# The first products of an all-expert layer as Strassen's seven block products over pairs of token chunks

## The chip, the cores and the metric

The kernel runs on one core of one Trainium2 chip. The metric is the time of the whole launch on the device, in microseconds (us), as the median of several runs. The engines are called PE (TensorE, matrix products), ACT (ScalarE), DVE (VectorE), POOL (GpSimd) and SP (SyncE, which issues most DMAs). PEld is PE's weight load, which runs beside its matmuls.

## What is computed

Three layers, one after the other: windowed attention with a linear bias, a layer in which each token goes to one of eight experts of limited capacity, and a layer in which each token goes through all of four experts. The change touches the last one:

```python
# x: [2304, 512], p: [2304, 4], w1: [4, 512, 1024], w2: [4, 1024, 512]
p = domain_probs / (domain_probs.sum(-1, keepdims=True) + 1e-09)
out = np.zeros((N, D), dtype=np.float32)
for e in range(E):
    h = np.maximum(x @ w1[e], 0.0)
    out += p[:, e:e + 1] * (h @ w2[e])
```

`x @ w1[e]` are the first products here, `h @ w2[e]` the second products.

## The kernel before

**A product in three.** PE multiplies in a reduced fp32 format (fp32r). So each fp32 matrix is kept as a high and a low part: ACT rounds to the high part, and POOL or DVE subtracts it from the whole to get the low part. `mm3` then issues three matmuls, high x high, high x low and low x high, into one PSUM bank.

**Stages.** Attention runs to about 155 us, the routed layer with its eight groups (`grp[g]`, 288 tokens each) to about 610 us, the all-expert layer from 621 us on. Through the group stage a planner sets the order: each piece of work is a `step(name, engine, us, function, needs, rank)`, and `arranged` lays the steps on the engines by their needs, assumed lengths and ranks. The tokens' vectors y of the routed layer go to `y_dram`, as a high and a low part (`out_y`, L1013). Part of the all-expert layer is done inside the group stage, as fill: the first six of eight hidden tiles of expert 0 (`NFF = 6`; tiles `hp_f`, `po_f`; results `pt`, kept in `part_dram`, L1075 and L1082). Also there, eight pieces of the next stage's weights are loaded and split on ACT and DVE (`next w`).

**The turn.** The step `turn` closes the group stage's pools and opens the pool for the columns: `columns` loads y back from `y_dram` (L1107), and `sums` loads what `part_dram` holds as the first value of the sums `acc` (L1111). All tokens' columns (`yTh`, `yTl`) and all sums then stay in SBUF.

**The all-expert stage.** The remaining 26 hidden tiles of 128 are seven units, `UNITS` = (expert, first tile, tiles): six units of four tiles and one of two. The outer loop goes over the units, the inner over six chunks of `CH = 384` tokens. For each chunk, `hid_mm` makes each of the unit's hidden tiles (`hp_b`: four steps of 128 rows, three matmuls each), `hid_up` (L800) evicts the relu of it on ACT as the high part, `hid_lo` (L803) the low part on DVE; then `combine` makes the second products of the chunk before (`po`, 128 tokens x 512) and adds them to `acc` on DVE, times the token's share (L1211). Two weight pieces of the next unit are split with every chunk, high on ACT (L755), low on POOL (L760), so each weight is split once. In the last unit each finished block of 128 tokens is scattered to its rows by a DMA from POOL's queue (L1213). In this stage PE and ACT follow the order in which the code is written (`tc.manual_schedule`); DVE, POOL and SP are ordered by the scheduler.

Of the kernel before, what the change touches and what calls it, by code (L numbers as in the profile page):

```python
# [25 lines left out]
def fused_kernel(ctx: ExitStack, tc: tile.TileContext, q, k, v, w_gate, w1, w2, probs, m2w1, m2w2, out, dbg=None):  # L26
# [27 lines left out]
    y_dram = dram.tile([P, 2, NK, NT], F32, name="y_dram")  # L54
# [470 lines left out]
    wp = ctx.enter_context(tc.tile_pool(name="wp", bufs=2))  # L525
# [203 lines left out]
    jobs, raws = [], []  # L729

# [59 lines left out]
    def mm3(o, ah, al, bh, bl, first, last):  # L790
        T.matmul(o, ah, bh, start=first, stop=False)  # L791
        T.matmul(o, ah, bl, start=False, stop=False)  # L792
        T.matmul(o, al, bh, start=False, stop=last)  # L793
# [95 lines left out]
    def pieces(n, job_of, known, free, names):  # L889
        nonlocal npieces  # L890
        for j in range(n):
            i = npieces
            npieces += 1
            raw = {}
            step(
                ("load", i), SP_, 0.5, lambda j=j, raw=raw: raw.update(r=load_piece(job_of(j))),
                [known, ("low", i - NRAW) if i >= NRAW else None, ("load", i - 1) if i else None], 3,
            )
            step(
                ("up", i), ACT_, 0.54, lambda j=j, raw=raw: upper_piece(job_of(j), raw["r"]),  # L900
                [(("load", i), LAND), free(j), ("up", i - 1) if i else None], 3,
            )
            step(("low", i), DVE_, 0.6, lambda j=j, raw=raw: lower_piece(V, job_of(j), raw["r"]), [("up", i), ("low", i - 1) if i else None], 3)
            names.append(("low", i))
# [23 lines left out]
    for g in range(E):  # L928
# [8 lines left out]
        for c in range(NK):  # L937
            def rows(g=g, c=c):
# [12 lines left out]
                [("rows", g, c), (("out", g - 1), 5.0) if g else None], 1,  # L951
# [30 lines left out]
        for i in range(NK):  # L982
            for f in range(2 * NFH):
                hf, ff = f // NFH, f % NFH

                def outputs(g=g, i=i, f=f, hf=hf, ff=ff):
                    d = grp[g]
                    if f == 0:
                        d["yp", i] = ps_y.tile([P, 512], F32, tag="y", name=f"y_{g}_{i}")
                    (wh, wl), (hh, hl) = d["w", hf][1][0], d["h", hf]  # L990
                    dsl = slice(i * P, (i + 1) * P)
                    mm3(d["yp", i][:, :CAP], wh[:, ff, dsl], wl[:, ff, dsl], hh[:, ff, :CAP], hl[:, ff, :CAP], f == 0, f == 2 * NFH - 1)
                step(
                    ("y", g, i, f), PE_, 0.41, outputs,
                    [prev_pe, ("hl", g, hf, ff), names[8 + f], bank(banks_y, 2, ("yl", g, i)) if f == 0 else None], 3,
                )
# [93 lines left out]
    CH = 384  # L1090
    NCH = NT // CH
    yT, accs = [None] * NCH, [None] * NCH
    accp = []

    def late_pool(name, side, columns_of, sums_of):
        pool = ctx.enter_context(tc.tile_pool(name=name, bufs=1, side=side, reuse_waits="tile"))
        accp.append(pool)
        for ch in columns_of:
            yT[ch] = [pool.tile([P, NK, CH], F32R, name=f"yT{n}_{ch}") for n in "hl"]
        for ch in sums_of:  # L1100
            accs[ch] = pool.tile([P, CH // P, DM], F32, name=f"acc_{ch}")

    def columns(ch):

        cs = slice(ch * CH, (ch + 1) * CH)
        for n in range(2):
            nc.sync.dma_start(yT[ch][n].bitcast(F32), y_dram[:, n, :, cs])  # L1107
# [8 lines left out]
    pieces(  # L1116
        8, lambda j: (w0["n"][0][1] + w0["n"][1][1])[j], ("next w",),
        lambda j: ("hid", E - 1, 0, NFH - 1, NK - 1) if j < 4 else ("y", E - 1, NK - 1, 2 * NFH - 1), [],
    )

    def turn():
        rctx.close()
        hctx.close()
        late_pool("acca", "right", range(4), range(1))

    step(("turn",), SP_, 0.0, turn, [("first h", E - 1, NFF - 1, NK - 1), ("fl", E - 1, NFF - 1), ("out", E - 1), ("keep", E - 1), ("gather", E - 1)], 1)
    for ch in range(2):
        step(("columns", ch), SP_, 0.8, lambda ch=ch: columns(ch), [("turn",), (("out", E - 1), 6.0)], 2)
# [59 lines left out]
    late_pool("accb", "left", range(4, NCH), range(1, NCH))  # L1188
    sums(0)
    for ch in range(2, NCH):  # L1190
        columns(ch)
        sums(ch - 1)
    sums(NCH - 1)


# [4 lines left out]
    done, stores = [], []  # L1200

    def combine(u, ch, w, h):
        e, _, nf = UNITS[u]
        for i in range(CH // P):
            t = ch * (CH // P) + i
            po = ps_y.tile([P, 512], F32, tag="y", name=f"po_{u}_{t}")
            ts_ = slice(i * P, (i + 1) * P)
            for f in range(nf):
                mm3(po, h[0][:, f, ts_], h[1][:, f, ts_], w[2][:, f, :], w[3][:, f, :], f == 0, f == nf - 1)
            pe = pp[:, t, e : e + 1]  # L1210
            V.scalar_tensor_tensor(accs[ch][:, i, :], po, pe, accs[ch][:, i, :], ALU.mult, ALU.add)  # L1211
            if u == len(UNITS) - 1:
                st = G.indirect_dma_start(  # L1213
                    out=out, out_offset=bass.IndirectOffsetOnAxis(ap=ids[:, t : t + 1], axis=0),
                    in_=accs[ch][:, i, :], in_offset=None,
                )
                for other in stores:
                    tc.declare_no_dep(st.ins, other.ins, reason="rows of other tokens")
                stores.append(st)

    ctx.enter_context(tc.manual_schedule(engines={mybir.EngineType.PE, mybir.EngineType.Activation}))
    unit = w0["n"]
    for u, (_, _, nf) in enumerate(UNITS):
        w = unit[0][0] + unit[1][0]
        for ch in range(NCH):
            h = [accp[0].tile([P, NFH, CH], F32R, tag=f"h{n}", name=f"h{n}_b{u}_{ch}", bufs=2) for n in "hl"]
            for f in range(nf):
                hp = ps_h.tile([P, 512], F32, tag="h", name=f"hp_b{u}_{ch}_{f}")
                for c in range(NK):
                    hid_mm(hp, w[:2], yT[ch], f, c, CH)  # L1230
                hid_up(hp, h, f, CH)
                hid_lo(hp, h, f, CH)
            done.append((u, ch, w, h))
            if len(done) > 1:
                combine(*done[-2])

            if ch == 0 and u + 1 < len(UNITS):
                unit = all_w(*UNITS[u + 1])
                jobs.extend(unit[0][1] + unit[1][1])
            for _ in range(min(2, len(jobs))):  # L1240
                split_piece()
# [29 lines left out]
```

## Time and profile before

| | us |
|---|---|
| runs | 1284.18, 1284.43, 1285.84 |
| median | 1284.43 |
| the profiled execution | 1281.37 |
| its span (first to last instruction) | 1279.7 |
| PE busy in it | 1224.9 |
| DVE, ACT, POOL busy | 633.8, 403.8, 216.6 |

The rows come from the profiled execution, so sums are made against 1281.37. An engine's busy time counts its own instructions; a matmul's duration in the timeline overlaps the next one's, so a pace is read from the starts.

### The profile page before, as it was taken

What the parts mean: (1) busy time and instruction counts of PE and PEld (TensorE: products, weight loads), DVE (VectorE), ACT (ScalarE), POOL (GpSimd) and SP (SyncE); (2) the same over time, 40 slices, a digit from 0 to 9 for tenths busy, and PEclk for the clock granted to TensorE, in tenths of its full rate; (3) what the DMA queues carried; (4) which work ended last, traced back from release to release, by engine and by line L of the source; (5) the groups of instructions that cost most, each with busy time, mean ns of one, the idle gap of its engine ahead of it and who ended that gap; (6) DMA issues with size and microseconds to landing.
All of it is one profiled execution on the core that took longest, in us unless ns stands there. A gap on an engine that the chain in (4) does not pass through costs nothing.

```text
span 1279.7 us, 21264 instructions
## 1 busy us (share of the span) xinstructions
PE 1224.9 (96%) x8209; PEld 1108.0 (87%) x8209; DVE 633.8 (50%) x1828; ACT 403.8 (32%) x1041; POOL 216.6 (17%) x264
## 2 busy tenths in 40 slices
PE   7999828999999999999999999999999999999998
PEld 6998817888889899999999889889999998888896
DVE  6999888898868564433122243222222222222222
ACT  8998733433233243433211112111111111111110
POOL 8867500100000000000100111101101100100112
PEclk9999957999999999999999999999999999999999
DMA  9653144544444253544940111101100000000111
GB/s 182 150 144 76 51 150 101 172 121 111 133 139 148 74 161 109 164 136 121 324 179 1 33 34 33 33 1 33 32 2 17 34 17 17 9 1 1 41 42 66
DMA packets 125012, 108.58 MB, mean 85 GB/s; under 512 B 76272, under 2 KB 91632, under 8 KB 124912
## 3 DMA queue, kind: packets, MB, share of 16 engines
q1 hardware_dynamic: 121936, 97.76, 26.9%
q0 software_dynamic: 2976, 9.48, 2.2%
q8 instruction: 64, 1.05, 0.3%
q14 instruction: 36, 0.29, 0.1%
HBM read 83.53 MB, written 23.68 MB: 84 GB/s over the span
## 4 chain that ended last, share of the span: by engine, by line
PE 69%; DVE 10%; issue 5%; DMA 2%; POOL 1%; ACT 0%; POOLq 0%; SPq 0%; DVEq 0%; ACTq 0%
PE hp_b L791 8%; PE hp_b L793 8%; PE hp_b L792 8%; PE po L791 8%; PE po L793 8%; PE po L792 7%; PE hp_a L791 2%; PE hp_a L792 2%; PE hp_a L793 2%; PE po_f L791 2%; DMA raw_a<-in_moe_w_dram 2%; DVE wl_a L760 2%; PE y L791 2%; PE po_f L792 2%; PE po_f L793 2%
## 5 line engine op out<-in xcount | busy, mean ns | idle before, releaser
L800 ACT ACTIVATE hh_b<-hp_b 128x384 fp32r<-128x384 f32 x156 | 76.6, 491 | 535.9 <-PE hp_b L793 535.9
L803 DVE SCALAR_TENSOR_TENSOR hl_b<-hp_b,hh_b 128x384 fp32r<-128x384 f32 x156 | 87.0, 558 | 263.9 <-ACT hh_b L800 263.9
L793 PE MATMUL hp_b<-yTh,wl_b 128*128 128x384 f32 x624 | 209.6, 336 | 0.0
L791 PE MATMUL hp_b<-yTh,wh_b 128*128 128x384 f32 x624 | 209.6, 336 | 0.0
L792 PE MATMUL hp_b<-yTl,wh_b 128*128 128x384 f32 x624 | 209.4, 336 | 0.0
L1211 DVE SCALAR_TENSOR_TENSOR acc<-po,pp,acc 128x512 f32<-128x512 f32 x126 | 94.6, 751 | 219.0 <-PE po L793 219.0
L791 PE MATMUL po<-wh_b,hh_b 128*128 128x512 f32 x468 | 184.8, 395 | 0.0
L793 PE MATMUL po<-wh_b,hl_b 128*128 128x512 f32 x468 | 184.7, 395 | 0.0
L792 PE MATMUL po<-wl_b,hh_b 128*128 128x512 f32 x468 | 184.7, 395 | 0.0
L760 POOL TENSOR_TENSOR wl_b<-raw_b,wh_b 128x512 fp32r<-128x512 f32 x44 | 56.0, 1291 | 536.2 <-ACT wh_b L755 439.8
L791 PEld LDWEIGHTS hp_b<-yTh,wh_b 128*128 128x128 f32 x624 | 117.3, 188 | 1.8
L792 PEld LDWEIGHTS hp_b<-yTl,wh_b 128*128 128x128 f32 x624 | 117.3, 188 | 1.7
L793 PEld LDWEIGHTS hp_b<-yTh,wl_b 128*128 128x128 f32 x624 | 117.3, 188 | 0.0
L793 PEld LDWEIGHTS po<-wh_b,hl_b 128*128 128x128 f32 x468 | 87.8, 188 | 21.3
L792 PEld LDWEIGHTS po<-wl_b,hh_b 128*128 128x128 f32 x468 | 87.8, 188 | 19.5
L791 PEld LDWEIGHTS po<-wh_b,hh_b 128*128 128x128 f32 x468 | 87.7, 187 | 19.4
L760 DVE TENSOR_TENSOR wl_a<-raw_a,wh_a 128x512 fp32r<-128x512 f32 x128 | 84.0, 682 | 2.3 <-ACT wh_a L755 1.7
L721 POOL DMA_INDIRECT xg<-x_dram,idx x24 | 24.5, 1019 | 356.0 <-DMA p_dram<-xg 55.1
L755 ACT CAST wh_a<-raw_a 128x512 fp32r<-128x512 f32 x128 | 72.6, 619 | 29.8 <-DMA raw_a<-in_moe_w_dram 29.5
L791 PE MATMUL hp_a<-xh,wh_a 128*128 128x288 f32 x256 | 80.4, 314 | 0.0
L791 PE MATMUL y<-hh_a,wh_a 128*128 128x288 f32 x256 | 78.3, 306 | 0.5 <-DVE yl L1006 0.3
L792 PE MATMUL hp_a<-xl,wh_a 128*128 128x288 f32 x256 | 76.4, 298 | 0.0
(219 smaller groups left out, 2502.5 us busy)
## 6 DMA issues: line engine op xcount, KB each, us to landing
raw_a<-in_moe_w_dram SPq DMA_DIRECT2D x128, 256.0 KB, 3.7
raw_b<-in_moe_w_dram SPq DMA_DIRECT2D x64, 256.0 KB, 2.7
x_dram<-x SPq DMA_DIRECT2D x18, 258.0 KB, 2.5
y_dram<-yh SPq DMA_DIRECT2D x8, 576.0 KB, 3.1
y_dram<-yl SPq DMA_DIRECT2D x8, 576.0 KB, 4.8
yTh<-y_dram SPq DMA_DIRECT2D x6, 768.0 KB, 9.5
yTl<-y_dram SPq DMA_DIRECT2D x6, 768.0 KB, 11.0
acc<-part_dram SPq DMA_DIRECT2D x6, 768.0 KB, 11.2
```

The costliest lines, as they stand in the source:

```text
L721: G.indirect_dma_start(out=xg[:, j, :], out_offset=None, in_=x_dram[:, :], in_offset=bass.IndirectOffsetOnAxis(ap=d["idx"][:, j : j + 1], ...
L755: S.copy(res[n][0][0][:, a, b], raw)
L760: eng.tensor_tensor(lo[:, a, b], raw, hi[:, a, b].bitcast(F32), ALU.subtract)
L791: T.matmul(o, ah, bh, start=first, stop=False)
L792: T.matmul(o, ah, bl, start=False, stop=False)
L793: T.matmul(o, al, bh, start=False, stop=last)
L800: S.activation(h[0][:, f, :n], hp[:, :n], AF.Relu)
L803: V.scalar_tensor_tensor(h[1][:, f, :n], hp[:, :n], 0.0, h[0][:, f, :n].bitcast(F32), ALU.max, ALU.subtract)
L1211: V.scalar_tensor_tensor(accs[ch][:, i, :], po, pe, accs[ch][:, i, :], ALU.mult, ALU.add)
```

## The change

The first products of the all-expert stage are regrouped. Two chunks of 384 tokens form a pair, and a product of a unit is read as a 2x2 block product: the hidden tiles in two halves, the 512 rows of the contraction in two halves, the pair's two chunks. Strassen's scheme makes it from seven products of sums and differences of blocks instead of eight products of blocks. The outer loop is now over the three pairs, the inner over the units, there and back, which gives 21 turns. The seven products of a turn accumulate in three kinds of PSUM banks (`m1`, `m2`, `m3`), and behind each stands one block of 128 tokens of the second products of the turn before (`second_products`); six such blocks, so the seventh product has none behind it.

What is prepared: per pair, `token_work` loads four blocks of y, makes four sums or differences of them (`t1` to `t4`) on DVE, and splits seven operands (ACT and DVE, 768 columns). Per unit within a pair, `weight_work` loads four blocks of w1, makes `s1` to `s4` on POOL, splits seven operands (ACT high, POOL low), and loads and splits the second weights (`vh`, `vl`; ACT and POOL). At the two changes of the pair the unit stays the same, so its weights are used again; 19 of the 21 turns have new ones. The part of the preparation with slot i is written behind product i of the turn before. For the first turn it is steps of the planner behind the step `turn`.

What else goes with it: `y_dram` holds y once, in fp32, for which ACT makes a copy `ys`; the steps `next w` and `columns` are gone; `wp` and two PSUM pools now close at the turn; `acc` has three buffers and is loaded pair by pair.

```diff
-    y_dram = dram.tile([P, 2, NK, NT], F32, name="y_dram")
+    y_dram = dram.tile([P, NK, NT], F32, name="y_dram")
...
+                    d["ys"] = fw.tile([P, NK, CAP], F32, tag="ys", name=f"ys_{g}")
...
+            step(("ys", g, i), ACT_, 0.42, lambda g=g, i=i: S.copy(grp[g]["ys"][:, i, :], grp[g]["yp", i][:, :CAP]), [("yh", g, i), (("out", g - 1), 5.0) if g else None], 2)
...
-            for n in range(2):
-                nc.sync.dma_start(y_dram[:, n, :, g * CAP : (g + 1) * CAP], grp[g]["y"][n].bitcast(F32))
-        step(("out", g), SP_, 1.0, out_y, [(("yl", g, NK - 1), 0.5)], 2)
+            nc.sync.dma_start(y_dram[:, :, g * CAP : (g + 1) * CAP], grp[g]["ys"])
+        step(("out", g), SP_, 0.6, out_y, [(("ys", g, NK - 1), 0.3), ("yl", g, NK - 1)], 2)
...
-    step(("next w",), SP_, 0.0, start_w("n", lambda: all_w(*UNITS[0])), [("load", npieces - 1)], 1)
...
-    for ch in range(2):
-        step(("columns", ch), SP_, 0.8, lambda ch=ch: columns(ch), [("turn",), (("out", E - 1), 6.0)], 2)
...
+        l = {kj: load(*kj) for kj in ((0, 0), (1, 1), (0, 1), (1, 0))}
+        x0 = split(0, (0, 0), [l[0, 0]])
+        t3 = less("t3", (1, 1), (0, 1), ALU.subtract, [l[1, 1], l[0, 1]], 0)
+        t1 = less((0, 1), (0, 1), (0, 0), ALU.subtract, [t3, l[0, 0]], 0)
+        t2 = less((0, 0), "t3", (0, 0), ALU.add, [t1, x0], 1)
+        split(1, (0, 0), [t2])
+        x2 = split(2, (1, 0), [l[1, 0]])
+        split(3, "t3", [t2])
+        split(4, (0, 1), [t1])
+        t4 = less((1, 0), (1, 0), (0, 0), ALU.subtract, [x2, t2], 5)
+        split(5, (1, 0), [t4])
+        split(6, (1, 1), [t3])
...
+        l = {ik: load(*ik) for ik in ((0, 0), (1, 0), (1, 1), (0, 1))}
+        x0 = split(0, (0, 0), [l[0, 0]])
+        s1 = less("s1", (1, 0), (1, 1), ALU.add, [l[1, 0], l[1, 1]], 0)
+        s3 = less((1, 0), (0, 0), (1, 0), ALU.subtract, [s1, l[0, 0]], 0)
+        s2 = less((0, 0), "s1", (0, 0), ALU.subtract, [s3, x0], 1)
+        split(1, (0, 0), [s2])
+        x2 = split(2, (0, 1), [l[0, 1]])
+        split(3, (1, 0), [s3])
+        split(4, "s1", [s2])
+        split(5, (1, 1), [s1])
+        s4 = less((0, 1), (0, 1), (0, 0), ALU.subtract, [x2, s2], 6)
+        split(6, (0, 1), [s4])
+        for f in range(nf):
+            second_piece(f)
...
+    first = {}
+    for what, (todo, made) in (("t", token_work(0)), ("w", weight_work(0, "0"))):
+        first[what] = made
+        for i, (eng, us, fn, needs, _) in enumerate(todo):
+            lands = [(((what, j)), LAND) if todo[j][0] == SP_ else (what, j) for j in needs]
+            step((what, i), eng, us, fn, [("turn",), *lands], 3)
...
+        product(0, 1, True)
+        s1 = {}
+        for f in range(nh):
+            s1[f] = temp("s1", f)
+            S.copy(s1[f], m[1, f][:, :CH])
+        yield
+        product(1, 2, True)
+        u2 = plus("u2", 2, s1)
+        yield
+        product(2, 1, False)
+        result({f: m[1, f] for f in range(nh)}, 0, 0)
+        yield
+        product(3, 2, False)
+        u3 = plus("u3", 2, s1)
+        yield
+        product(4, 3, True)
+        result(plus("cs", 3, u3), 1, 1)
+        yield
+        product(5, 2, False)
+        result(plus("cs", 2, s1), 1, 0)
+        yield
+        product(6, 3, False)
+        result(plus("cs", 3, u2), 0, 1)
+        yield
...
+        for i, _ in enumerate(first_products(u, pair, w[0], x, h, str(n))):
+            next(before_, None)
+            for slot, fn in work:
+                if slot == i:
+                    fn()
```

In this cut `product(i, bank, new)` issues 2 x 3 matmuls for each of the unit's `nh` tiles of one half into bank `m1`, `m2` or `m3`, either anew or onto what it holds; `plus` is a DVE sum of a bank and an SBUF tile; `result(a, i, j)` is `hid_up` and `hid_lo` for half i of chunk j.

The order of the instructions shows where this stands on two engines. In the names, the last numbers only tell tiles apart; `pt_7_1` and `pt_7_2` are the last evictions of the group stage's fill, `hh_b0_0` those of the first unit. On ACT at the turn, before:

```order
L1075 ACTIVATE pt_7_1_9710<-po_f7_1_9684,ppf_7_1_9339 128x512
L1075 ACTIVATE pt_7_2_9728<-po_f7_2_9706,ppr_7_9342 128x512
L800 ACTIVATE hh_b0_0_9768<-hp_b0_0_0_9770 128x384
L800 ACTIVATE hh_b0_0_9768<-hp_b0_0_1_9785 128x384
L800 ACTIVATE hh_b0_0_9768<-hp_b0_0_2_9800 128x384
L800 ACTIVATE hh_b0_0_9768<-hp_b0_0_3_9815 128x384
```

The same place on ACT after the change (`xh` the seven token operands, `wh0_0` the first weight operand of turn 0):

```order
L1063 ACTIVATE pt_7_1_9725<-po_f7_1_9683,ppf_7_1_9357 128x512
L1118 CAST xh2_0_9730<-b10_0_9676 128x768
L1118 CAST xh6_0_9738<-b11_0_9669 128x768
L1118 CAST xh4_0_9747<-b01_0_9671 128x768
L1118 CAST xh1_0_9755<-b00_0_9662 128x768
L1063 ACTIVATE pt_7_2_9763<-po_f7_2_9719,ppr_7_9360 128x512
L1118 CAST xh3_0_9765<-t3_0_9723 128x768
L1118 CAST xh5_0_9773<-b10_0_9676 128x768
L1162 CAST wh0_0_9777<-a00_0_9681 128x512
```

Six token casts and the first weight cast now stand behind or between the evictions `pt`. A little further on ACT after the change, from turn 0's second copy `s1` to its first evictions `hh` (`wh0_1`, `wh1_1`, `wh2_1` are operands of turn 1):

```order
L1335 COPY s1_0_1_9864<-m1_0_1_9855 128x384
L1162 CAST wh6_0_9812<-a01_0_9703 128x512
L1174 CAST vh2_0_9821<-w2raw2_0_9816 128x512
L1174 CAST vh3_0_9825<-w2raw3_0_9819 128x512
L1162 CAST wh0_1_9874<-a00_1_9866 128x256
L1162 CAST wh1_1_9900<-a00_1_9866 128x256
L787 ACTIVATE hh_0_0_9844<-m1_0_0_9848 128x384
L787 ACTIVATE hh_0_0_9844<-m1_0_1_9855 128x384
L1162 CAST wh2_1_9920<-a01_1_9872 128x256
```

Five weight casts stand ahead of the two `hh` of product 2, the last of them of the next turn's sums. On POOL behind the group stage's last gather, before:

```order
L760 TENSOR_TENSOR wl_b06_0_9839<-raw_b06_0_0_0_9830,wh_b06_0_9838 128x2x256
L760 TENSOR_TENSOR wl_b06_0_9839<-raw_b06_0_2_0_9832,wh_b06_0_9838 128x2x256
L760 TENSOR_TENSOR wl_b06_1_9949<-raw_b06_1_0_0_9834,wh_b06_1_9948 128x512
L760 TENSOR_TENSOR wl_b06_1_9949<-raw_b06_1_1_0_9836,wh_b06_1_9948 128x512
L760 TENSOR_TENSOR wl_b14_0_10455<-raw_b14_0_0_0_10444,wh_b14_0_10454 128x512
```

And after the change (`L1155` the sums of weight blocks, where `s2` overwrites `a00` and `s4` overwrites `a01`; `L1164` and `L1177` the low parts):

```order
L1155 TENSOR_TENSOR s1_0_9742<-a10_0_9689,a11_0_9694 128x512
L1155 TENSOR_TENSOR a10_0_9689<-a00_0_9681,a10_0_9689 128x512
L1164 TENSOR_TENSOR wl0_0_9778<-a00_0_9681,wh0_0_9777 128x512
L1155 TENSOR_TENSOR a00_0_9681<-s1_0_9742,a00_0_9681 128x512
L1164 TENSOR_TENSOR wl2_0_9782<-a01_0_9703,wh2_0_9781 128x512
L1164 TENSOR_TENSOR wl1_0_9801<-a00_0_9681,wh1_0_9800 128x512
L1164 TENSOR_TENSOR wl3_0_9787<-a10_0_9689,wh3_0_9786 128x512
L1164 TENSOR_TENSOR wl4_0_9804<-s1_0_9742,wh4_0_9803 128x512
L1164 TENSOR_TENSOR wl5_0_9790<-a11_0_9694,wh5_0_9789 128x512
L1155 TENSOR_TENSOR a01_0_9703<-a01_0_9703,a00_0_9681 128x512
L1177 TENSOR_TENSOR vl0_0_9794<-w2raw0_0_9708,vh0_0_9793 128x512
L1164 TENSOR_TENSOR wl6_0_9813<-a01_0_9703,wh6_0_9812 128x512
```

Before, POOL's first work here belonged to the second unit; now it is the first turn's own weights, one operation after another.

## Rows read from the trace of the kernel before

**Rows 1.** Of the page: the span, and busy us (share) xinstructions of each engine

```profile
span 1279.7 us, 21264 instructions
PE 1224.9 (96%) x8209; PEld 1108.0 (87%) x8209; DVE 633.8 (50%) x1828; ACT 403.8 (32%) x1041; POOL 216.6 (17%) x264
```

**Rows 2.** Groups by line: xcount | busy us, mean ns | idle before, releaser

```profile
L793 PE MATMUL hp_b<-yTh,wl_b 128*128 128x384 f32 x624 | 209.6, 336 | 0.0
...
L793 PE MATMUL po<-wh_b,hl_b 128*128 128x512 f32 x468 | 184.7, 395 | 0.0
...
L800 ACT ACTIVATE hh_b<-hp_b 128x384 fp32r<-128x384 f32 x156 | 76.6, 491 | 535.9 <-PE hp_b L793 535.9
...
L803 DVE SCALAR_TENSOR_TENSOR hl_b<-hp_b,hh_b 128x384 fp32r<-128x384 f32 x156 | 87.0, 558 | 263.9 <-ACT hh_b L800 263.9
...
L1211 DVE SCALAR_TENSOR_TENSOR acc<-po,pp,acc 128x512 f32<-128x512 f32 x126 | 94.6, 751 | 219.0 <-PE po L793 219.0
...
L760 POOL TENSOR_TENSOR wl_b<-raw_b,wh_b 128x512 fp32r<-128x512 f32 x44 | 56.0, 1291 | 536.2 <-ACT wh_b L755 439.8
...
L760 DVE TENSOR_TENSOR wl_a<-raw_a,wh_a 128x512 fp32r<-128x512 f32 x128 | 84.0, 682 | 2.3 <-ACT wh_a L755 1.7
...
L755 ACT CAST wh_a<-raw_a 128x512 fp32r<-128x512 f32 x128 | 72.6, 619 | 29.8 <-DMA raw_a<-in_moe_w_dram 29.5
```

**Rows 3.** Timeline of PE at both ends of the stage; start us, duration us

```profile
620.76 0.39 PE L793 MATMUL po_f<-wh_b,restl 128*128 128x512 f32 x1
620.99 0.34 PE L791 MATMUL hp_b<-yTh,wh_b 128*128 128x384 f32 x1
...
1272.92 0.40 PE L793 MATMUL po<-wh_b,hl_b 128*128 128x512 f32 x1
```

**Rows 4.** Timeline of PE within that stage, first products and second products

```profile
700.35 0.33 PE L791 MATMUL hp_b<-yTh,wh_b 128*128 128x384 f32 x1
...
700.87 0.33 PE L791 MATMUL hp_b<-yTh,wh_b 128*128 128x384 f32 x1
...
705.21 0.40 PE L791 MATMUL po<-wh_b,hh_b 128*128 128x512 f32 x1
...
705.91 0.39 PE L791 MATMUL po<-wh_b,hh_b 128*128 128x512 f32 x1
```

**Rows 5.** Timeline of SP's queue and a window (columns as in Rows 7) at the turn

```profile
608.52 0.38 SPq L1107 DMA_DIRECT2D yTh<-y_dram  x1
...
613.00:615.00 2.00, 2.00 (x11) 1.61 (x10) 0.00 (x0) 0.51 (x1) 0.00 (x0) 1.00 1.03 362
```

**Rows 6.** Timeline of ACT at the turn; in brackets the idle time before

```profile
616.99 0.69 ACT L1075 ACTIVATE pt<-po_f,ppf 128x512 f32<-128x512 f32 x1 [3.47 <-PE po_f L793]
621.19 0.69 ACT L1075 ACTIVATE pt<-po_f,ppr 128x512 f32<-128x512 f32 x1 [3.51 <-DMA part_dram<-pt]
```

**Rows 7.** Windows: busy us (instructions) by engine, granted clock, DMA

```profile
core 0: us, PE busy (x) PEld busy (x) DVE busy (x) ACT busy (x) POOL busy (x), PEclk, DMA share, GB/s
...
160.00:165.00 5.00, 1.30 (x19) 1.01 (x19) 3.63 (x13) 1.24 (x2) 0.00 (x0) 0.64 0.78 254
200.00:205.00 5.00, 5.00 (x25) 4.53 (x24) 4.45 (x14) 1.96 (x5) 0.00 (x0) 0.50 0.45 131
205.00:210.00 5.00, 5.00 (x40) 4.61 (x39) 3.48 (x11) 2.14 (x5) 0.00 (x0) 0.92 0.63 36
```

**Rows 8.** The same windows view, for the middle of the group stage

```profile
200.00:560.00 360.00, 352.14 (x2710) 320.49 (x2709) 256.28 (x763) 129.96 (x290) 20.89 (x21) 0.99 0.43 129
```

**Rows 9.** Line 457 (min/median/max ns), then DVE's and POOL's timelines at 96 us

```profile
L457 DVE TENSOR_SCALAR rs<-sums x36: 156/393/726, 14.1 to 153.7; 128x4 f32<-128x4 f32 x36
...
96.49 1.15 DVE L122 TENSOR_TENSOR eq<-logits,m 128x72 f32<-128x72 f32 x1
...
96.26 1.28 POOL L350 TENSOR_TENSOR vl<-v,vh 128x512 fp32r<-128x512 f32 x1
```

More of the change, by code (lines that the diff above doesn't have):

```diff
@@ L788, in all_w, with mm3 @@
         )
[L790 to L793, printed above, removed]
+    def mm3(o, ah, al, bh, bl, first, last, onto=False):
+        kept = dict(skip_group_check=True) if onto else {}
+        T.matmul(o, ah, bh, start=first, stop=False, **kept)
+        T.matmul(o, ah, bl, start=False, stop=False, **kept)
+        T.matmul(o, al, bh, start=False, stop=last, **kept)
     def hid_mm(hp, w, x, f, c, n):
@@ L950, in fused_kernel @@
                 ("xh", g, c), ACT_, 0.42, lambda g=g, c=c: S.copy(grp[g]["x"][0][:, c, :], grp[g]["tp", c][:, :CAP]),
-                [("rows", g, c), (("out", g - 1), 5.0) if g else None], 1,
+                [("rows", g, c)], 1,
             )
@@ L994, in fused_kernel @@
                     ("y", g, i, f), PE_, 0.41, outputs,
-                    [prev_pe, ("hl", g, hf, ff), names[8 + f], bank(banks_y, 2, ("yl", g, i)) if f == 0 else None], 3,
+                    [prev_pe, ("hl", g, hf, ff), names[8 + f], bank(banks_y, 2, ("ys", g, i)) if f == 0 else None], 3,
                 )
@@ L1090, in fused_kernel @@
     CH = 384
[L1091 to L1107, printed above, removed]
@@ L1121, in turn, with late_pools @@
-    def turn():
+    NPAIR = NT // (2 * CH)
+    ORDER = ("11", "s2t2", "12", "s3t3", "s1t1", "a22t4", "s4b22")
+    UNITS = [(1, 0, NFH), (0, NFF, 2 * NFH - NFF), (1, NFH, NFH)] + [(e, f, NFH) for e in range(2, E2) for f in (0, NFH)]
+    dp = {}
+    def late_pools():
         rctx.close()
         hctx.close()
-        late_pool("acca", "right", range(4), range(1))
-    step(("turn",), SP_, 0.0, turn, [("first h", E - 1, NFF - 1, NK - 1), ("fl", E - 1, NFF - 1), ("out", E - 1), ("keep", E - 1), ("gather", E - 1)], 1)
@@ new lines, in fused_kernel @@
+    step(("turn",), SP_, 0.0, late_pools, [("first h", E - 1, NFF - 1, NK - 1), ("fl", E - 1, NFF - 1), ("out", E - 1), ("keep", E - 1), ("gather", E - 1)], 1)
+    first = {}
[4 more added lines that the diff above has]
+            step((what, i), eng, us, fn, [("turn",), *lands], 3)
@@ L1187, in fused_kernel @@
     fctx.close()
[L1188 to L1193, printed above, removed]
+    dl = ctx.enter_context(tc.tile_pool(name="dl", bufs=1, reuse_waits="tile"))
     ids = moe.tile([P, NTL], I32, name="ids")
@@ L1199, in fused_kernel @@
     nc.sync.dma_start(pp, p_dram.rearrange("(t p) e -> p t e", p=P))
-    done, stores = [], []
-    def combine(u, ch, w, h):
-        e, _, nf = UNITS[u]
[L1204 to L1241, printed above, removed]
@@ L1242, in fused_kernel, with sums, second_products @@
-    combine(*done[-1])
+    ctx.enter_context(tc.manual_schedule(engines={mybir.EngineType.PE, mybir.EngineType.Activation}))
+    stores, accs = [], {}
+    def sums(ch):
+        cs = slice(ch * CH, (ch + 1) * CH)
+        accs[ch] = dl.tile([P, CH // P, DM], F32, tag="acc", name=f"acc_{ch}", bufs=3)
+        nc.sync.dma_start(accs[ch], part_dram[cs, :].rearrange("(t p) d -> p t d", p=P))
+    def second_products(u, pair, second, h, last):
+        e, _, nf = UNITS[u]
+        for j in range(2):
+            ch = 2 * pair + j
+            for i in range(CH // P):
+                t = ch * (CH // P) + i
+                po = ps_y.tile([P, 512], F32, tag="y", name=f"po_{u}_{t}")
+                ts_ = slice(i * P, (i + 1) * P)
+                for f in range(nf):
+                    mm3(po, h[j][0][:, f, ts_], h[j][1][:, f, ts_], second[f][0], second[f][1], f == 0, f == nf - 1)
+                pe = pp[:, t, e : e + 1]
+                V.scalar_tensor_tensor(accs[ch][:, i, :], po, pe, accs[ch][:, i, :], ALU.mult, ALU.add)
+                if last:
+                    st = G.indirect_dma_start(
+                        out=out, out_offset=bass.IndirectOffsetOnAxis(ap=ids[:, t : t + 1], axis=0),
+                        in_=accs[ch][:, i, :], in_offset=None,
+                    )
+                    for other in stores:
+                        tc.declare_no_dep(st.ins, other.ins, reason="rows of other tokens")
+                    stores.append(st)
+                yield
@@ L1246 @@
+    for _ in before_:
+        pass
 _INS = ['q', 'k', 'v', 'moe_w_gate', 'moe_w1', 'moe_w2', 'moe2_domain_probs', 'moe2_w1', 'moe2_w2']
```

143 lines of the change are left out of this document (119 added, 24 removed).

## The prediction, made before the changed kernel had run

> **What bounds the kernel now.** First the page: in a span of 1279.7 us PE is busy 1224.9, 96% [rows 1]. Then the groups by line: the first products of the all-expert stage (hp_b, three times 624 matmuls) and its second products (po, three times 468) show no idle time before them, while the eviction on ACT (hh_b) waited 535.9 us for PE [rows 2]. Next the bounds of the stage on PE: the last group-stage matmul is followed by the first hp_b at 620.99 without a gap, and the last po starts at 1272.92 [rows 3]. The pace there: from 700.35 to 700.87 three hp_b matmuls, 0.52/3 = 0.1735 us each; from 705.21 to 705.91 three po matmuls, 0.2333 each [rows 4]. Check: 1872 x 0.1735 + 1404 x 0.2333 = 324.8 + 327.6 = 652.4 us, which is 620.99 to 1273.3. So this stage is matmul count times pace and nothing else; PE at a granted clock of 1.00 is its only limit, and only fewer matmuls shorten it.
>
> **What is removed.** Strassen leaves seven block products of eight: 1872 x 7/8 = 1638 matmuls of 384 columns. 234 x 0.1735 = **40.6 us** off PE. The second products keep their count and shape. The new matmuls have the same 128x128 weights and 384 columns, so I keep the pace.
>
> **The steady state of the new loop.** There are 21 turns (7 units x 3 token pairs). A full turn is 7 x 2 x 2 x 3 = 84 first and 6 x 4 x 3 = 72 second matmuls: 14.6 + 16.8 = 31.4 us of PE. A short turn comes three times, and the mean over 21 is (284.2 + 327.6)/21 = 29.1. Against that, per full turn:
> POOL: 4 sums and 11 splits of 128x512, 1.291 us each as in the wl_b row [rows 2]: 19.4 us. Weights were split once, 44 pieces on POOL in the whole stage; now 19 of 21 turns prepare theirs.
> DVE: 10 sums out of PSUM and 8 hl, each at the hl_b row's 0.558, and 6 acc at 0.751: 14.6 us; at the two pair changes some 10 more for token blocks (11 operations of 768 columns; the wl_a row's 0.682 for 512 gives 1.0 at most, I take 0.9).
> ACT: 11 weight casts at 0.619, 8 hh and 2 copies at 0.491: 11.7 us.
> All stay below 29.1, POOL as the nearest with 10 us to spare, and PE's order puts a chunk of second products (2.8 us) behind each product (2.1 us), which covers the 1.05 us from a product's end through hh and hl, or 1.6 us with the sum before them. So I cost these at nothing; the cover is gone if one POOL operation takes over 29.1/15 = 1.94 us.
>
> **The first turn is not covered, and this is the large cost.** Before, the split weights of the first unit were ready at the turn: they lay in the group stage. Now token loads, weight loads, sums and splits start at the turn step, where the column loads started, 608.52 [rows 5]. PE still has 12.4 us of the last po_f until 620.99.
> Loads: four token blocks of 393 KB, four weight blocks of 256 KB, then part_dram and two second pieces, 2.6 to 3.2 MB. At 362 GB/s, what the column loads moved [rows 5], that is 7 to 9 us: landed by 616 to 619. Not the limit.
> ACT's hand-written order is. The cast wh0 stands behind pt_7_2, which ran at 621.19 for 0.69 us [rows 6] (its row names a DMA as releaser, but PE's last po_f ended only at 621.15 [rows 3]), and behind two token casts of 768 columns. From 0.619 for 512 [rows 2] I take 0.88 for 768 (bounds 0.62 and 0.93). So wh0 ends at 621.88 + 1.76 + 0.62 = 624.3, wl0 on POOL 625.6; behind it POOL works one piece after another at 1.29 (s2, wl2, wl1 at 629.5, ... s4 634.6, vl0 635.9, wl6 637.2, vl1 638.5). Product 1 needs wl1, so it ends at about 631 and product 6 at 641.4, against 635.5 had PE gone on from 620.9: 5.9 us lost.
> Then ACT again: hh of product 2 stands behind wh6, vh2, vh3 and the next unit's wh0 and wh1. vh3 wants a load whose buffer vl1 frees at 638.5; wh0 of the next turn a load behind acc, 768 KB, about 644; wh1 the fourth of four POOL operations of 256 columns, which at 0.73 (between half of 1.29 and the whole) end at 647.3. Then hh and hl, 648.8. Only then is a PSUM bank free for turn 1's first product. Its product and the first chunk, which also needs hh of product 5 (two slots further in ACT's queue), end at about 654.7; undisturbed this would be 620.9 + 14.6 + 1.0 + 2.8 = 639.3. Lost: **15.4 us**.
> Clock: PE then stands for several us at a time. After PE was busy 1.30 of 5 us the granted clock was 0.64; with PE full at 200 to 205 it was 0.50 and then 0.92 in the next 5 [rows 7]. Half speed for the first 5 us and 0.8 of the next 5 (0.92) loses **2.9 us**; bounds 0 (the waits here may leave the clock alone) and 5.8 (twice).
> Sum 18.3 us. From below: 4 us, if the order of the casts delays only the first product (624.3 less 620.9). From above: 30, if each of the 19 POOL operations that stand in a row takes 0.6 us more.
>
> **Other edits.** In the group stage y is stored once instead of as hi and lo: 16 stores of 576 KB become 8, ACT gets 32 copies (under the hh_b row's 0.491, since they have 288 columns; inside waits of ACT for PE), the eight weight pieces for the next stage leave DVE. PE is busy 352.1 of 360 us there [rows 8], so at most 8 us could come back, and none of the edits takes a matmul out. The planner's order on PE changes a little: 0, bounds -4 to +4. If the ACT copies hold up the evictions, a y bank comes free later, and that is inside these 4. The tail after the last po, 1272.92 to 1279.7, keeps its scatter of six chunks: 0.
>
> **Sum.** -40.6 + 18.3 = -22.3. The profiled execution took 1281.37, of which the span is 1279.7; it is 3.06 under the median of the runs, 1284.43. So 1259.1 for the profiled one, **1262.1** for the median.
>
> **Rivals.**
> *The first turn is mostly hidden.* If ACT's casts come through sooner than I read the queue (the pt waits shorter, the loads for turn 1 ahead of acc) only the late start is lost, 4 us: -36.6, 1248. For it: DVE and POOL are idle at the turn, and the loads land before PE ends. Against: ACT's order is fixed by hand, and pt_7_2 waits for PE.
> *Small stalls in each turn.* POOL's chain and ACT's queue couple turns: hl of the last products, or wh1 ahead of hh, may keep PE 0.3 to 0.7 us a turn. 21 x 0.5 = 10.5: 1272.5. For: hh of product 2 stands behind the next wh1, which waits for three POOL sums. Against: these have 10 us of slack in a turn of 29.
> *POOL becomes the bound, and it is slower.* The rows show DVE and POOL in each other's way: a DVE operation that has both inputs in SBUF, 128x72, took 1.15 us and ended 0.1 us after the POOL operation that began before it; and a 128x4 one took from 156 to 726 ns [rows 9]. If this also works the other way, so that each POOL operation waits for one DVE operation of 0.751, it costs 1.291 + 0.75 = 2.04 us, 15 of them 30.6, over the deciding 29.1. With 1.5 us x 19 turns = 29 more: 1291. Against: in that same row the POOL operation kept its 1.28 us; it was DVE that paid, and 14.6 us of DVE in 29.1 can bear it; of its 24 operations a turn only the six hl that read the sums have both inputs in SBUF.
> The Trainium skill, page "Advanced Engine Details and Errata", section "VectorE Performance Modes", says that the second SBUF port of Vector is shared with GPSIMD and that the instructions "will interfere/block eachother". The 1.15 us row bears out the blocking of DVE; that POOL is blocked in turn, no row shows. By the rule in both directions the time would be that of this rival; by the row alone it stays at the forecast.
> *It does less than it says.* Accumulating onto a bank that already holds a product might cost PE time: the same products at 0.198 instead of 0.1735 would use up the seven eighths, and with the first turn's 18 the time would be 1303. No row shows PE slower for what a bank holds: of the three matmuls from 700.35 to 700.87 [rows 4] two add to what the first left, and they keep the pace. I give it 0.01.
>
> **How the numbers follow.** Forecast (first turn 12 to 24): 1256 to 1268, 0.55. Hidden: 1244 to 1256, 0.15. Small stalls: 1268 to 1281, 0.17. No change, within 0.2% (1281.9 to 1287.0, about what a measurement of this kernel can tell from none): 0.04. Slower: 0.09, of which POOL's case 0.08. Faster is 0.55 + 0.15 + 0.17 = 0.87. For 8 in 10 the range takes the forecast, most of the hidden case and most of the small stalls: 1247 to 1279, leaving out the 0.13 above, some 0.03 of the stalls and 0.04 below.
>
> **What would show it.** The new stage on PE should show 284 + 328 us of matmuls at 0.1735 and 0.2333, clock 1.00; between the last po_f and about 655 us PE should stand some 7 + 7 us, the first wait ended by ACT's wh0 and POOL's wl, the second by DVE's hl behind wh1 of turn 1; later turns show POOL busy near 19.4/31.4 and no idle PE. Wrong if POOL operations average over 1.94 us, if PE waits in every turn, or if the first wait is missing.

## The result, and the profile after

| | us | runs |
|---|---|---|
| before | 1284.99 | 1284.18 to 1285.84 |
| after | 1264.07 | 1262.44 to 1268.1 |
| predicted | 1262.1 | 1247 to 1279 |

The ratio is 0.9842, 95% interval 0.9816 to 0.9867: faster, by 20.9 us where 22.3 was forecast (before is now the median of four runs; the forecast went by the first three, 1284.43). The profiled execution of after took 1262.44, where 1259.1 was forecast; 2.7 of these 3.3 us are the later end of the group stage in it, which a repeat below shows to be scatter.

The page of after, as [rows 1]:

```profile
span 1260.7 us, 22085 instructions
...
PE 1192.1 (95%) x7975; PEld 1075.0 (85%) x7975; DVE 779.9 (62%) x2048; ACT 524.8 (42%) x1284; POOL 508.4 (40%) x499
```

PE has 234 matmuls less; POOL has more than twice its work. What PE waited for from 600 us to the end, as the waits view sums it (us in total, times, longest):

```profile
PE m L778 <- DVE hl L790: 8.2, 1, 8.2
PE m L778 <- ACT wh L1162: 2.7, 1, 2.7
PE m L780 <- POOL wl L1164: 1.0, 1, 1.0
```

Three waits, 12.0 us, the last of them ahead of turn 1's first product. In PE's timeline (the counterpart of [rows 3]) they stand here; after them PE waits no more until the last `po`:

```profile
623.46 0.40 PE L780 MATMUL po_f<-wh_b,restl 128*128 128x512 f32 x1
626.61 0.69 PE L778 MATMUL m<-xh,wh 128*128 128x384 f32 x1 [2.75 <-ACT wh L1162]
...
628.62 0.69 PE L780 MATMUL m<-xh,wl 128*128 128x384 f32 x1 [1.00 <-POOL wl L1164]
629.11 0.52 PE L778 MATMUL m<-xh,wh 128*128 128x384 f32 x1
629.43 0.52 PE L779 MATMUL m<-xl,wh 128*128 128x384 f32 x1
...
653.21 0.69 PE L778 MATMUL m<-xh,wh 128*128 128x384 f32 x1 [8.22 <-DVE hl L790]
653.69 0.53 PE L779 MATMUL m<-xl,wh 128*128 128x384 f32 x1
654.01 0.53 PE L780 MATMUL m<-xh,wl 128*128 128x384 f32 x1
...
658.48 0.40 PE L780 MATMUL po<-vh,hl 128*128 128x512 f32 x1
...
707.37 0.35 PE L780 MATMUL m<-xh,wl 128*128 128x384 f32 x1
707.56 0.34 PE L778 MATMUL m<-xh,wh 128*128 128x384 f32 x1
...
1253.99 0.40 PE L780 MATMUL po<-vh,hl 128*128 128x512 f32 x1
```

After each of the two long waits the matmuls start 0.32 us apart for some us, not 0.17 (629.11 and 629.43; 653.69 and 654.01): the lower level of the clock. The windows view has it as a granted clock of 0.83 in both stretches (columns as in [rows 7]), and 1.00 from 660 on:

```profile
620.00:640.00 20.00, 16.25 (x74) 14.53 (x73) 12.88 (x15) 11.18 (x19) 13.29 (x9) 0.83 0.43 139
640.00:660.00 20.00, 11.78 (x55) 10.74 (x53) 7.61 (x14) 7.58 (x19) 13.54 (x16) 0.83 0.63 211
...
800.00:900.00 100.00, 100.00 (x496) 89.58 (x496) 58.73 (x86) 32.38 (x61) 51.91 (x41) 1.00 0.30 93
```

The `po` row at 658.48 is the last of the first chunk (one block of 128 tokens) of second products. ACT's timeline, the counterpart of [rows 6], shows why PE stood:

```profile
623.90 0.69 ACT L1063 ACTIVATE pt<-po_f,ppr 128x512 f32<-128x512 f32 x1 [0.59 <-PE po_f L780]
624.48 0.82 ACT L1118 CAST xh<-t 128x768 fp32r<-128x768 f32 x1
625.21 0.83 ACT L1118 CAST xh<-b 128x768 fp32r<-128x768 f32 x1
625.94 2.18 ACT L1162 CAST wh<-a 128x512 fp32r<-128x512 f32 x4
...
648.26 0.40 ACT L1162 CAST wh<-a 128x256 fp32r<-128x256 f32 x1 [2.27 <-DMA a<-in_moe_w_dram]
651.77 0.40 ACT L1162 CAST wh<-a 128x256 fp32r<-128x256 f32 x1 [3.11 <-POOL a L1155]
652.08 0.86 ACT L787 ACTIVATE hh<-m 128x384 fp32r<-128x384 f32 x2
```

The first weight cast comes behind `pt` and two token casts at 625.94; `hh` of product 2 (652.08), whose accumulation had ended before 637, stands behind turn 1's two casts, of which the first waited 2.27 us for its load and the second 3.11 us for POOL's sum.

Two lengths are used below, both between starts of matmuls: the **stretch** from the last `po_f` to the last `po`, and its **first part** up to the twelfth `po`, the end of the first chunk. Undisturbed, the first part would be 0.23 (the last `po_f`) + 14.57 (84 matmuls of turn 0) + 1.04 (six of turn 1's first product) + 11 x 0.2333 = 18.4 us.

### The profile page after: what moved, and what is told of

It reads as the page before. It is cut to its first block, busy times and chain, and to the rows that moved or that the text cites. A ratio compares the mean times of both kernels' runs of the same rounds, so it can differ in the third digit from the quotient of the medians.

```text
span 1260.7 us, 22085 instructions
## 1 busy us (share of the span) xinstructions
PE 1192.1 (95%) x7975; PEld 1075.0 (85%) x7975; DVE 779.9 (62%) x2048; ACT 524.8 (42%) x1284; POOL 508.4 (40%) x499
## 4 chain that ended last, share of the span: by engine, by line
PE 67%; DVE 9%; issue 4%; DMA 4%; POOL 2%; ACT 1%; SPq 0%; POOLq 0%; DVEq 0%; ACTq 0%
PE po L779 8%; PE po L780 8%; PE po L778 8%; PE m L780 7%; PE m L779 7%; PE m L778 7%; PE hp_a L778 2%; PE hp_a L780 2%; PE hp_a L779 2%; PE po_f L778 2%; DMA raw_a<-in_moe_w_dram 2%; PE po_f L779 2%; PE po_f L780 2%; PE y L778 2%; DVE wl_a L758 2%
## 5 line engine op out<-in xcount | busy, mean ns | idle before, releaser
L778 PE MATMUL m<-xh,wh 128*128 128x384 f32 x546 | 184.4, 338 | 11.0 <-DVE hl L790 8.2
L780 PE MATMUL m<-xh,wl 128*128 128x384 f32 x546 | 185.7, 340 | 1.0 <-POOL wl L1164 1.0
L780 PE MATMUL po<-vh,hl 128*128 128x512 f32 x468 | 185.7, 397 | 0.0
L779 PE MATMUL po<-vl,hh 128*128 128x512 f32 x468 | 185.6, 397 | 0.0
L779 PE MATMUL m<-xl,wh 128*128 128x384 f32 x546 | 185.6, 340 | 0.0
L778 PE MATMUL po<-vh,hh 128*128 128x512 f32 x468 | 185.2, 396 | 0.0
L1164 POOL TENSOR_TENSOR wl<-a,wh 128x512 fp32r<-128x512 f32 (+1 forms) x114 | 140.3, 1237 | 83.9 <-ACT wh L1162 83.8
L1177 POOL TENSOR_TENSOR vl<-w2raw,vh 128x512 fp32r<-128x512 f32 x70 | 94.6, 1354 | 100.2 <-ACT vh L1174 100.2
L778 PEld LDWEIGHTS m<-xh,wh 128*128 128x128 f32 x546 | 103.6, 190 | 17.1 <-DVE hl L790 8.5
L779 PEld LDWEIGHTS m<-xl,wh 128*128 128x128 f32 x546 | 103.4, 189 | 5.6
L780 PEld LDWEIGHTS m<-xh,wl 128*128 128x128 f32 x546 | 103.7, 190 | 1.6 <-POOL wl L1164 1.5
```

Of the source, the lines that this page charges most:

```text
L778: T.matmul(o, ah, bh, start=first, stop=False, **kept)
L779: T.matmul(o, ah, bl, start=False, stop=False, **kept)
L780: T.matmul(o, al, bh, start=False, stop=last, **kept)
L1164: todo.append((POOL_, 1.3, lambda: G.tensor_tensor(out[i][1], raw[a], out[i][0].bitcast(F32), ALU.subtract), [len(todo) - 1], i))
L1177: todo.append((POOL_, 1.3, lambda: G.tensor_tensor(second[f][1], raw["w", f], second[f][0].bitcast(F32), ALU.subtract), [len(todo) - 1], 8 ...
```

## The experiments

**One eighth left out of the kernel before.** What are the matmuls worth alone?

```diff
-                for c in range(NK):
-                    hid_mm(hp, w[:2], yT[ch], f, c, CH)
+                kept = NK - 1 if f < nf // 2 else NK
+                for c in range(kept):
+                    ...
```

> The kernel before, with one eighth of the first products of the all-expert stage left out (of the four contraction steps the last one, for half of each unit's hidden tiles): 234 matmuls of 384 columns fewer, nothing else changed, no sums, no repeated weight work. Theory A (the stage is matmul count times pace; what the change loses against its 40.6 us it loses at the first turn): 234 x 0.1735 = 40.6 us less, about 1244, stage 611.8 us long with no wait of PE. Theory B (the pace is not free to hold once ACT and DVE have less time per chunk, so that the 40.6 us are never there): 1250 or more, with waits of PE for hl or hh. The group stage in this profile is a second sample of before's, to compare with the 2.7 us later end of the changed kernel's: if that is the run's own scatter this one may differ by as much; if it is the planner's order it ends near 621 again.

Measured: ratio 0.9700 (0.9672 to 0.9728); stretch 1229.26 - 617.66 = 611.6 us, against 652.2 before. That is 40.6 to the tenth, with no wait of PE: theory A, and the first term of the sum. The changed kernel has the same number of PE instructions, 7975, and a stretch of 630.5; so its 18.9 us above 611.6 are what the change costs beside its matmuls.

**The changed kernel a second time.**

> The changed kernel itself, a second time, on the chip of the next three runs. What is compared is the stretch from the end of the last po_f to the end of the last po: 630.5 us in its first profile, 652.2 in the profile of before, 611.6 with an eighth left out. If that stretch repeats within 1 us while the point at which the group stage ends moves again (617.4 to 623.7 in the six profiles so far), the 2.7 us by which the group stage ended later is scatter and not the change's.

Measured: ratio 0.9849 (0.9829 to 0.987), stretch 630.7, first part 35.2 against 35.0. The last `po_f` started at 619.82, and not at 623.46. Over the ten profiles with the group stage of the changed kernel it started from 617.2 to 623.5 (mean 620.7), in the two with that of before at 620.8 and 617.7. So the 2.7 us by which this stage ended later in the first profile are scatter of an execution; a cost of 1 or 2 us in it can't be told from that. Hence stretches are compared below, not only times.

**The order of the first turn, one point at a time.** First only `hh` ahead of turn 1's casts:

```diff
-                if slot == i:
+                if (max(slot, 2) if n == 0 else slot) == i:
                     fn()
```

> The changed kernel; only in the first turn the weight work of slots 0 and 1 (for turn 1) is written behind the evictions of product 2, so that ACT has hh ahead of wh0 and wh1 of turn 1. Theory A1 (PE's 8.2 us wait comes from hh standing behind wh1 in ACT's queue): the bank is free at about 639, but turn 1's own wh0 then waits for its load, which landed at 648.3 in the changed kernel, and wl0 for 649.5; so the wait shrinks from 8.2 to about 4 us and its releaser changes to ACT wh or POOL wl: 4 to 5 us less, 1259. Theory A2 (the chain of POOL operations is what PE really waits for, ACT's order only shows it): under 1.5 us less. Theory B (losses in each turn): no change.

Measured: ratio 0.9859 (0.983 to 0.9889), stretch 632.0, first part 35.1: nothing gained. PE's waits, in the same view:

```profile
PE m L778 <- ACT wh L1162: 5.8, 2, 3.1
PE po L778 <- ACT hh L787: 2.5, 1, 2.5
PE m L780 <- POOL wl L1164: 1.4, 1, 1.4
```

The wait for `hl` is gone, as theory A1 said, but turn 1's `wh` and then `hh` of a later product came last in its place. The waits are 9.7 us in all instead of 12.0, but the granted clock was 0.50 from 650 to 660 us, where the changed kernel had 0.50 and 0.84 in these two windows of 5 us. The order on ACT was one of several things that arrived together.

Then the first turn's steps in another order for the planner: weights ahead of tokens, or both by need:

```diff
-    for what, (todo, made) in (("t", token_work(0)), ("w", weight_work(0, "0"))):
+    for what, (todo, made) in (("w", weight_work(0, "0")), ("t", token_work(0))):
```

> The changed kernel; only the planner is given the first turn's weight steps ahead of its token steps. wh0 then stands behind the first of the last three evictions pt (about 616) and not behind the last (624), so POOL's row of first-turn operations begins some 8 us earlier. Theory A (the row of POOL operations, started too late by ACT's order, sets the first turn): first wait of PE under 1 us, product 6 ends near 641, turn 1's first product starts near 643 and its first chunk ends near 647 instead of 658.7: 10 to 13 us less, about 1252. If the loads set it (weights landing, the second pieces' two buffers, the load of turn 1 behind acc), the start moves but the 8.2 us wait stays: 4 us less, 1260. Theory B: no change.

```diff
...
+    for _, what, i, eng, us, fn, lands in sorted(steps, key=lambda s: s[0]):
+        step((what, i), eng, us, fn, [("turn",), *lands], 3)
```

> The changed kernel; only the planner is given the first turn's weight and token steps merged in the order in which the products need them (slot 0 of both, slot 1 of both, ...; the second weights' pieces last). Theory A: POOL starts at about 617 and its operations come in the order of the products; product 0 at the end of the last po_f, one wait of about 0.5 us at product 1, then turn 1's first product near 639 to 640 without the clock having fallen: 13 to 16 us less, about 1249. If POOL's 19 operations in a row are too long whatever their order, 6 to 9 us less. Theory B: no change.

Measured: weights first, ratio 0.9827 (0.9797 to 0.9857), first part 31.6, stretch 631.3 (a later wait of 2.4 and a fall of the clock behind it took this back); by need, 0.9801 (0.9773 to 0.9829), first part 32.0, stretch 627.5. Both missed the 10 to 16 us expected. POOL's first `wl` did start 7 us before the last `po_f`, instead of 3 us behind it, but then (DVE's and POOL's timelines by need):

```profile
618.62 2.05 DVE L1111 TENSOR_TENSOR b<-b,b 128x768 f32<-128x768 f32 x1
...
622.55 5.90 DVE L1120 TENSOR_TENSOR xl<-b,xh 128x768 fp32r<-128x768 f32 x3
...
617.84 5.92 POOL L1164 TENSOR_TENSOR wl<-a,wh 128x512 fp32r<-128x512 f32 x3
...
625.67 1.98 POOL L1164 TENSOR_TENSOR wl<-s,wh 128x512 fp32r<-128x512 f32 x1
```

Here both engines worked without a pause of more than 0.4 us from 618 to 629 us, each beside the other's operations, and each operation in the two rows of three took 1.97 us on either engine. In the changed kernel, where the other engine stood still meanwhile, three of the same took:

```profile
629.88 3.76 POOL L1164 TENSOR_TENSOR wl<-a,wh 128x512 fp32r<-128x512 f32 x3
...
623.01 2.69 DVE L1120 TENSOR_TENSOR xl<-b,xh 128x768 fp32r<-128x768 f32 x3
```

That is 1.25 and 0.90 each. Beside each other they got little more done than one after the other would (2.15 us for a pair). Bringing POOL's row forward laid it on DVE's token row, and PE now waited 4.5 us for `xl`.

**More POOL work in every turn.** The rival of the prediction, tried directly:

```diff
-            todo.append((POOL_, 1.3, lambda: G.tensor_tensor(out[i][1], raw[a], ...
+            todo.append((POOL_, 1.3, lambda: [G.tensor_tensor(out[i][1], raw[a], ...) for _ in range(1 if key == "0" else 2)], ...
```

> The changed kernel; from turn 1's weights on each of the seven subtractions for wl is done twice (same operands, same result), so a full turn has 22 POOL operations instead of 15. By the mean of 1.31 us in the changed kernel's trace that is 28.8 us of POOL in a turn of 31.4 on PE. Theory A (POOL has 10 us of slack a turn): no steady stall, 0 to 8 us more in all, from turns 0 and 1. The rival of the prediction (POOL near its limit, 2.04 us an operation beside DVE): 45 us a turn, over 1450. In between: PE waits for wl in the full turns, a few us each, 1290 to 1330; then the slack is smaller than the sum of durations says.

Measured: ratio 1.0093 (1.0074 to 1.0113), 1292.7 us, stretch 663.1. My expectation of 0 to 8 us missed; by its time it is the case in between, but PE did not come to wait for `wl` in the full turns. By shape, from 660 us on, first the changed kernel and then this one (count, busy, mean ns):

```profile
L790 DVE SCALAR_TENSOR_TENSOR hl<-cs,hh 128x384 fp32r<-128x384 f32 x113 | 75.7, 678 | 11.5 <-ACT hh L787 5.7
...
L790 DVE SCALAR_TENSOR_TENSOR hl<-m,hh 128x384 fp32r<-128x384 f32 x37 | 20.4, 557 | 32.3 <-ACT hh L787 32.2
...
L1164 POOL TENSOR_TENSOR wl<-a,wh 128x512 fp32r<-128x512 f32 x90 | 117.6, 1311 | 55.2 <-ACT wh L1162 55.2
```

```profile
L790 DVE SCALAR_TENSOR_TENSOR hl<-cs,hh 128x384 fp32r<-128x384 f32 x111 | 120.9, 1119 | 11.2 <-ACT hh L787 7.9
...
L790 DVE SCALAR_TENSOR_TENSOR hl<-m,hh 128x384 fp32r<-128x384 f32 x37 | 19.4, 554 | 139.0 <-ACT hh L787 139.0
...
L1164 POOL TENSOR_TENSOR wl<-a,wh 128x512 fp32r<-128x512 f32 x180 | 247.7, 1379 | 24.0 <-ACT wh L1162 19.1
```

`hl` with both inputs in SBUF (`cs`, `hh`) went from 678 to 1119 ns; `hl` with one input in PSUM (`m`) stayed at 555; POOL rose by 5%. In this kernel PE waited ten times for `acc` on DVE, 20.4 us in all. But DVE's longer operations are not what these waits come from. The longest of them (ACT, DVE, PE):

```profile
698.16 0.62 ACT L1162 CAST wh<-a 128x512 fp32r<-128x512 f32 x1 [16.39 <-POOL a L1155]
...
699.20 1.02 DVE L790 SCALAR_TENSOR_TENSOR hl<-m,hh 128x384 fp32r<-128x384 f32 x2 [13.35 <-ACT hh L787]
...
700.94 0.79 PE L778 MATMUL po<-vh,hh 128*128 128x512 f32 x1 [6.77 <-DVE acc L1289]
```

ACT stood 16.39 us for POOL's sum with `hh` behind that cast, DVE stood 13.35 us for `hh` with `acc` behind `hl`, and PE waited for `acc`. It is so at all ten: just ahead of each ACT had stood 9 to 17 us for POOL's sum and DVE 8 to 13 us for `hh`. From 660 us on ACT waited 214.1 us for POOL's sums, against 80.3 in the changed kernel, and DVE 146.9 us for `hh`, against 37.9. So 22 POOL operations a turn cost what they cost through POOL's own row, passed on by ACT's order and DVE's, with POOL busy 76 to 89 of each 100 us from 660 to 1160. In the changed kernel it is 45 to 73, and PE does not wait.

**The first turn arranged by hand, on either engine.** Loads and the operands of products 0 to 2 in the order of need, operands of products 3 to 6 behind turn 0's products, turn 1's work from product 3 on; the weight sums and `wl` once on DVE (the diff), once on POOL:

```diff
+        who, by, took = (V, DVE_, 0.7) if key == "0" else (G, POOL_, 1.3)
...
+            if n == 0:
+                for fn in at_slot.get(i, []):
+                    fn()
-                if slot == i:
+                if (max(slot, 3) if n == 0 else slot) == i:
```

> The changed kernel with its first turn arranged anew: loads in the order of need; of the first turn's operands those of products 0 to 2 prepared by planner steps in the order of need, those of products 3 to 6 written behind the products of turn 0 like the later ones; the first turn's weight sums and wl on DVE (0.68 us) instead of POOL (1.29); turn 1's weight work not before product 3. Theory C (formed on the run by need: operations of DVE and POOL that have all operands in SBUF do not overlap; there both took about 1.97 us when they ran side by side, so all token and weight work of the first turn is one row): the row is 11 x 0.96 + 11 x 0.68 = 18 us and PE is served as it goes; PE waits 2 to 4 us in all, no long fall of the clock; stretch from last po_f to last po 615 to 618 us, 1250 on a chip where the changed kernel takes 1264. If only the order matters and not the engine, e10 gives the same.

> As the run before, but the first turn's weight sums and wl stay on POOL (order of need on each engine). Theory C (one port): 11 POOL operations of 1.29 and 11 token operations of 0.96 in one row, 25 us instead of 18: the operations of DVE in 610 to 630 take near 2 us, PE waits 5 to 8 us more than with DVE alone, 5 to 8 us slower than that run. Theory D (the two engines work beside each other and 1.97 us had another cause): the same time as the run before, or faster, since the work is shared by two engines.

Measured: DVE 0.9786 (0.9763 to 0.9809), stretch 624.1; POOL 0.9783 (0.9762 to 0.9805), 624.6. The first missed its 615 to 618 us. They are equal within the intervals, so theory C's 5 to 8 us between them is refuted, although its mechanism shows in the second (POOL's operations at 2.00 us from 626 to 632): the longer row fitted under PE's work. The longest wait left in both was one for `hh`, 2.5 and 3.5 us, behind turn 1's casts. The last pair moves these casts back, and two of the second pieces forward:

```diff
-                if (max(slot, 3) if n == 0 else slot) == i:
+                if (max(slot, 3 if slot == 0 else 5) if n == 0 else slot) == i:
...
-        at_slot.setdefault(2 + f, []).extend(...
+        at_slot.setdefault((2, 2, 4, 4)[f], []).extend(...
```

> The kernel of e10 (first turn in the order of need, its weight work on POOL), and in addition turn 1's wh1 to wh4 written behind the evictions hh of product 5, and the first turn's four second pieces ahead of turn 1's sums. In e10 PE's longest wait, 3.5 us, was the first chunk waiting for hh, which stood on ACT behind wh1 to wh3 of turn 1, and these behind POOL's third sum of turn 1 at 640; 1.0 more for hl. Theory A (what is left at the first turn are such orders, not a rate): both waits go, stretch 620 to 621 us instead of 624.6, about 1250. If POOL's row is the rate (the second pieces come late too): the first chunk still waits 2 us or more, now for vl or for hl, and the stretch stays over 623.

> The kernel of e9 (the same, with the first turn's weight sums and wl on DVE), changed in the same two points. Theory A: stretch 619 to 621 us. Since e9 and e10 agreed within 0.5 us, the engine should matter only if PE comes to wait for the row of operations itself; then this one, with 0.68 instead of 1.29 us for each of eleven, should be 1 to 3 us faster than e11.

Measured: POOL 0.9787 (0.9745 to 0.983), first part 23.0 instead of 28.3, stretch 621.8; DVE 0.9801 (0.9762 to 0.9839), 23.9 and 623.4. Both missed their expected stretches (620 to 621 and 619 to 621), and the second is not faster, against its expectation; in it the granted clock fell once more, to 0.66 from 660 to 665 us. PE's waits with POOL:

```profile
PE po L778 <- DVE acc L1308: 2.5, 1, 2.5
PE m L779 <- DVE xl L1120: 1.7, 2, 1.0
PE m L780 <- POOL wl L1165: 1.0, 2, 0.6
```

The first part gained 5.3 us, the stretch only 2.8: the 2.5 stand one turn later, at 660, where `acc` stood on DVE behind `hl`, this for `hh`, `hh` on ACT behind turn 2's `wh`, and that 6.12 us for POOL's sum:

```profile
650.46 0.62 ACT L1163 CAST wh<-a 128x512 fp32r<-128x512 f32 x1 [2.04 <-DMA a<-in_moe_w_dram]
...
657.72 0.62 ACT L1163 CAST wh<-a 128x512 fp32r<-128x512 f32 x1 [6.12 <-POOL a L1156]
658.25 0.48 ACT L787 ACTIVATE hh<-m 128x384 fp32r<-128x384 f32 x1
```

Turn 2's load was already late (ACT waited 2.04 us for it), and five POOL operations in a row came between its first cast and this one. So the first three turns' preparation is behind, and the place where PE feels it moves on with each repair. In total time the four can't be told apart (1253.9 to 1256.3 us); the two before the last pair have intervals (up to 0.9809) that end below those of the changed kernel (from 0.9816), so they are faster than both kernels, by about 0.6% than the changed one.

## Why the prediction was right, point by point

- **Removed, 40.6 us.** Right; the run with an eighth left out gave 40.6.
- **Steady state at no cost.** Nearly: from the twelfth `po` on the stretch is 595.5 us, matmul count times pace 593.4. The missing 2.1 us are no wait in the trace. Of the first matmuls of a product behind a chunk some start 0.18 to 0.19 apart instead of 0.17 (707.37 and 707.56), which makes 0.022 us at each of 120 such places, enough for the 2.1. Why is open.
- **First turn, 18.3 us.** The first part was 35.0 against 18.4: 16.6. Its split was off: 12.0 of waits where 15.4 stood, and so 4.6 of clock where 2.9 stood, since the clock fell twice (the upper bound was for that). In the stretch, 21.7 us shorter where the sum has 22.3, three misses nearly cancel: 3.4 us less of waits, 1.7 more of clock, 2.1 more in the steady state. That the total came so close is in part luck. The steps met the trace within 2 us when the later start, 2.7, is taken off: first product at 626.6 (forecast 624.3), turn 1's first at 653.2 (648.8), the first chunk's end 658.7 (654.7).
- **What decided it.** The prediction named ACT's order. The runs show that order as one of three limits that came due together: with it mended, the loads and sums of turn 1, then the token row on DVE, then turn 2's sums were late. The whole preparation of the first turn was too much for the 12 us left; no single queue was its cause.
- **Group stage 0, tail 0.** Held within the scatter; the tail was 6.7 us, as before.
- **The rivals.** Hidden (1248): no; the second long wait was there. Small stalls in each turn: no PE wait after 653. Less than it says: no; the products that add to a filled bank (the third, fourth and sixth of a turn) lose the same 0.022 us at their start as the second and fifth, which begin a bank. POOL the bound: not with 15 operations; with 22 its row was late, though an operation took 1.38 us and not 2.04. The Trainium skill, page "Advanced Engine Details and Errata", section "VectorE Performance Modes", says that GPSIMD instructions and "2p Vector instructions" block each other; the prediction left out the 2p, and no run here shows in which mode DVE's operations ran. Blocking the runs do show: both ways where both engines work from SBUF alone (1.97 us each), and nearly one way, DVE paying, where DVE's work is mixed (678 and 1119 against POOL's 1311 and 1379).

## What to carry to other kernels

A loop at matmul count times pace gives back exactly the matmuls that are taken out; the price of the preparation is then at the one place where no earlier work covers it, the first turn, and it is read there as a list of queues, not as one wait. Mending the wait that ends last shows the next one a few us later, so price the whole row first. Moving work to an idle engine may buy nothing if its operations and those of a busy one slow each other.

## What the hardware showed that was not expected

- DVE 128x768 and POOL 128x512 operations, both from SBUF alone, ran at 1.97 us each side by side, instead of 0.90 and 1.25 from start to start. DVE operations with one input in PSUM were not slowed (557 and 554 ns).
- Short waits left the clock alone in one run: in the last POOL arrangement PE stood five times up to 1.0 us between 628 and 644 and the granted clock was 1.00 in every 5 us window from 620 to 655. The wait of 2.5 us at 660 left it at 1.00 as well, while in the same arrangement with DVE the clock fell after one of 2.1 us there, so the length of the wait alone does not tell. With one wait of 3.5 us (the POOL arrangement before it) it was 0.95, then 0.50:

```profile
640.00:645.00 5.00, 1.64 (x8) 1.02 (x6) 2.76 (x5) 3.10 (x8) 4.48 (x6) 0.95 0.60 202
645.00:650.00 5.00, 3.83 (x7) 1.97 (x8) 5.00 (x6) 1.63 (x5) 4.84 (x4) 0.50 0.68 199
```
